# Linear attention fused with a capacity-routed mixture of experts: values loaded from ScalarE's queue, set-up work moved to VectorE's start, a new attention order, and digit counts folded by VectorE block transposes

## The chip, the cores and the metric

The kernel runs on one core of one Trainium2 chip. The metric is device time in microseconds (us) of one execution, given as the median of several runs; lower is better. The engines are PE (TensorE, matmuls; PEld is its weight load), DVE (VectorE), ACT (ScalarE), POOL (GpSimd) and SP (SyncE, which here only issues DMAs). A trailing q, as in SPq, marks DMA issues on that engine's queue. "Granted clock" is the share of TensorE's full clock that the profile records in a stretch; its two levels are 1.2 and 2.4 GHz, so 0.50 is the lower and 1.00 the upper one.

## The reference

Inputs: q, k, v of shape (8 batches, 8 heads, 576 positions, 64), a random-feature matrix w_phi (64 x 128), a gate (512 x 8) and the two weight matrices of 8 experts. What must be computed:

```python
def phi(x):
    proj = x @ w_phi
    proj = proj - max(abs(proj), axis=-1)
    return concat([exp(proj), exp(-proj)])
q_p, k_p = phi(q), phi(k)
kv  = einsum('bhsf,bhsd->bhfd', k_p, v);  z = k_p.sum(axis=2)
num = einsum('bhsf,bhfd->bhsd', q_p, kv); den = einsum('bhsf,bhf->bhs', q_p, z) + 1e-6
x = (num/den).transpose(0,2,1,3).reshape(4608, 512)
# routing: all 4608*8 logits in falling order; a token takes the expert of its highest
# logit whose expert is not yet full (576 tokens each)
logits = x @ w_gate
out[tokens of e] = maximum(x[tokens of e] @ w1[e], 0) @ w2[e]      # 512 -> 1024 -> 512
```

## The kernel before, in words

**Attention (0 to 296 us).** The 64 pairs of batch and head are worked in 16 units of four, u = 0 to 15 (two batches by two heads). Per unit SP issues 8 loads of k and 8 of q, 72 KB each (`raw` L115, its DMA line L122, called by `loadx`), two loads of v, 144 KB each (`loadv` L123, line L128), and one store of the finished block to `xs` in DRAM (L313). The loads write tiles with two buffers (`ki`, `qi`, `vi`). DVE turns k and q (`kT`, `qT`, L175); PE projects them (`g`, L186); DVE takes the row maximum (`kgm`, `qgm`, L190) and subtracts it (`kgt`, `qgt`, L193; two of the three k parts go by a copy on ACT L199 and a subtraction on POOL L202); ACT takes the exponentials (`kP`, L214). PE forms `kv` from `kP` and `vi` (L232), ACT copies it (`kvT` L236), PE spreads it by head (`bd` L248), and ACT copies it to `kz` (L251). POOL adds up the key features (`ks`, L222/L223), and PE and DVE place their sum in `kz` (L263, L265). PE transposes the query side (L276), ACT takes its exponentials (`qP`, L280), PE forms numerator and denominator ("num", L293), DVE divides (L297, L298, L308, tile `xp`), SP stores `xp`.

**What sets the order.** A planner written in Python, class `Plan` (L18), places every piece of a unit: each has an engine, a duration estimate, a due time, and buffer slots that it needs and frees. In the attention part each engine takes its pieces strictly by due time. The due times come from tables in the dictionary `ATT` (L913): `place` (L146) gives `u*16` plus the entry for the piece and engine from table '0' for the first unit, '1' for the second, '9' for the last and 's' for all between. The 19 pieces of set-up work for the routing (`init`, L336 to L342, which step through `moe_consts` L374: masks, iotas, selection matrices) have entries in table '0' that run from -103.6 to 91.2, so they lie scattered between the first units' work on DVE. The result of the planner is the program's order on each engine.

Each DMA goes on one of 8 completion lanes, given out in program order over all issuing engines; an issue first waits, on the engine that issues it, until the DMA before it on its lane has landed.

**Routing and experts (296 us to the end).** Routing finds, round by round, the expert that is filled next and the tokens that go to it. A round reads a 32-bit key in 6 digits (four of 5 bits, two of 6), from the top; for each digit it counts per expert how many tokens are at or above each of the K = 32 or 64 digit values, and finds the largest value at which the count still reaches the capacity. Round 0 is done in a wide form ahead of the experts. In rounds 1 to 6, which run beside the matmuls of experts 0 to 5, one digit is this chain: DVE compares (L586), PE counts with tokens packed n = 4 or 2 to a matmul (L602, 9 or 18 matmuls), DVE masks the packed result (`mm`, L604) and adds over n (`dd`, L606), PE adds over the n partition groups with a selection matrix (L609), DVE compares with the capacity (`fl`, L614), PE adds the flags over partitions (L616), DVE takes the digit (`ch`, L618) and moves to the next digit (`cc`, L622). The lines of one digit:

```python
mm=S([128,n,8],f'mm{n}'); V.tensor_mul(mm,p,msk[n])                     # L604
V.tensor_reduce(dd,mm.rearrange('p i e -> p e i'),axis=AX.X,op=OP.add)  # L606
p=rps([128,8]); PE.matmul(p,Q[n],dd[:,:,0],start=True,stop=True)        # L609
V.tensor_scalar(fl,p,float(cap),2.0**(-7*i),op0=OP.is_ge,op1=OP.mult)   # L614
p=rps([128,8]); PE.matmul(p,ones[0:KR],fl,start=True,stop=True)         # L616
```

An expert: weights arrive by DMA (`raww`, L736), ACT and DVE split them into a rounded part and a rest (`w1h` L804, `w1l` L807; `w2h`, `w2l` L808), POOL gathers the tokens (L819), PE transposes them (L824), then the two layers as three fp32r matmuls each (`h` L849, `y` L878 and L893) with ACT and DVE between (L860, L861, L864), and POOL scatters the result (L907). A second plan, with constants in `MOE` (L912), orders this part, the digits' steps with estimates from `steps` (L745).

Of the kernel before, what the change touches and what calls it, by code (L numbers as in the profile page):

```python
# [97 lines left out]
def attention(ctx, tc, nc, q, k, v, w_phi, w_gate, xs, L, C, xp, cfg={}, after=None, later=None, count=None, init=iter(())):  # L98
# [50 lines left out]
    def place(name,eng,u,due):  # L149
# [3 lines left out]
        return u*16.+t[{0:'0',1:'1',NU-1:'9'}.get(u,'s')][(name if isinstance(name,str) else ''.join(map(str,name)))+'.'+eng]  # L153
    def unit(u):
# [22 lines left out]
        def project(nm,g,s0,s1,due,src):  # L177
# [16 lines left out]
            add((nm,g),'PE',n*218.,due,pe,[(src[0]+'t',0),(src[0]+'t',1)],'Q',slots(('g',NG,nm,g)),((src,u),),ins=16*n+.5)  # L194
# [143 lines left out]
    for i in range(NI):  # L338
# [3 lines left out]
        P.add(('init',i),'DVE',330.,place(('init',i),'DVE',0,d['init']),some,[('init',i-1)] if i else [],lat=95.,after=3900.)  # L342
# [31 lines left out]
def moe_consts(rp, nc, C, L, MC, cfg={}):  # L374
# [599 lines left out]
```

## Time and profile before

| | |
|---|---|
| runs | 796.99, 798.92, 800.79 us; median 798.92 us |
| profiled execution | 796.87 us, span of its instructions 795.1 us, mean granted clock 0.978 |
| busy in the span | PE 750.4 us (94%), DVE 546.5 (69%), ACT 349.4 (44%), POOL 308.0 (39%) |
| attention, 0 to 296 us | 16 units |
| first routing round, 296 to 328 us | PE busy 20.1 of 32.4 us, granted clock 0.63 |
| experts 0 to 7, 328 us to the end | 62.6 us for expert 0; 57.6 to 58.8 for experts 1 to 5; 54.0 for expert 6 |

The span runs from the first to the last instruction; the execution's own time is 1.8 us longer. Busy shares are means over stages that have different limits, so each stage is to be read by itself.

### The profile page before, as it was taken

What the parts mean: (1) busy time and instruction counts of PE and PEld (TensorE: products, weight loads), DVE (VectorE), ACT (ScalarE), POOL (GpSimd) and SP (SyncE); (2) the same over time, 40 slices, a digit from 0 to 9 for tenths busy, and PEclk for the clock granted to TensorE, in tenths of its full rate; (3) what the DMA queues carried; (4) which work ended last, traced back from release to release, by engine and by line L of the source; (5) the groups of instructions that cost most, each with busy time, mean ns of one, the idle gap of its engine ahead of it and who ended that gap; (6) DMA issues with size and microseconds to landing.
All of it is one profiled execution on the core that took longest, in us unless ns stands there. A gap on an engine that the chain in (4) does not pass through costs nothing.

```text
span 795.1 us, 25101 instructions
## 1 busy us (share of the span) xinstructions
PE 750.4 (94%) x10718; PEld 651.2 (82%) x10718; DVE 546.5 (69%) x1343; ACT 349.4 (44%) x609; POOL 308.0 (39%) x327
## 2 busy tenths in 40 slices
PE   5999999899999986899999999999999999999995
PEld 3888888688888875598898898898898898897983
DVE  7998788598889857876686686685685685550400
ACT  2766667476766750343333333333333333441410
POOL 5887777688887850303203103104104104302011
PEclk9999999899999995899999999999999999999998
DMA  9767877867785311535505414423433334701200
GB/s 126 118 116 160 161 136 138 158 137 140 134 164 111 93 33 31 167 107 163 169 1 175 159 39 154 139 73 122 139 102 105 127 106 147 246 1 58 109 28 33
DMA packets 206655, 91.89 MB, mean 116 GB/s; under 512 B 154784, under 2 KB 189632, under 8 KB 206544
## 3 DMA queue, kind: packets, MB, share of 16 engines
q1 hardware_dynamic: 195712, 70.74, 37.5%
q0 software_dynamic: 6096, 18.97, 7.1%
q8 instruction: 84, 1.38, 0.7%
q10 hardware_dynamic: 4736, 0.59, 0.7%
q14 instruction: 27, 0.22, 0.1%
HBM read 71.39 MB, written 18.87 MB: 114 GB/s over the span
## 4 chain that ended last, share of the span: by engine, by line
PE 69%; issue 13%; DVE 5%; POOL 4%; SPq 3%; DMA 3%; ACT 1%; POOLq 0%; DVEq 0%; ACTq 0%
PE h L849 20%; PE y L878 17%; PE g L293 7%; PE g L232 7%; PE g L186 6%; SPq L122 3%; PE g L276 3%; PE y L893 2%; PE h L824 2%; POOL out_dram L907 1%; PE rps L602 1%; DMA qi<-in_q_dram 1%; POOL ks L223 1%; PE rps L598 1%; PE g L248 1%
## 5 line engine op out<-in xcount | busy, mean ns | idle before, releaser
L223 POOL TENSOR_TENSOR ks<-ks,kP 128x512 f32<-128x512 f32 x112 | 143.3, 1279 | 9.1 <-ACT kP L214 0.6
L849 PE MATMUL h<-xh,w1h 128*128 128x272 f32 (+3 forms) x512 | 144.5, 303 | 0.2 <-DVE xl L827 0.2
L849 PE MATMUL h<-xh,w1l 128*128 128x272 f32 (+3 forms) x512 | 142.9, 299 | 0.0
L907 POOL DMA_INDIRECT out_dram<-ysb,idx x40 | 40.4, 1010 | 206.2 <-ACT ysb L901 166.6
L860 ACT ACTIVATE fh<-h 128x272 fp32r<-128x272 f32 (+2 forms) x128 | 49.2, 384 | 134.7 <-PE h L849 123.6
L819 POOL DMA_INDIRECT xg<-xs,idx x40 | 39.5, 986 | 177.2 <-issue 141.3
L878 PE MATMUL y<-w2h,fl 128*128 128x512 f32 x256 | 102.1, 399 | 0.0
L878 PE MATMUL y<-w2l,fh 128*128 128x512 f32 x256 | 101.9, 398 | 0.0
L878 PE MATMUL y<-w2h,fh 128*128 128x512 f32 x256 | 101.3, 396 | 0.0
L849 PEld LDWEIGHTS h<-xh,w1h 128*128 128x128 f32 x512 | 96.4, 189 | 2.1 <-issue 1.2
L849 PEld LDWEIGHTS h<-xh,w1l 128*128 128x128 f32 x512 | 96.6, 189 | 0.0
L849 PE MATMUL h<-xl,w1h 128*128 128x272 f32 (+3 forms) x512 | 91.7, 298 | 0.0
L864 DVE SCALAR_TENSOR_TENSOR fl<-h,fh 128x272 fp32r<-128x272 f32 (+2 forms) x128 | 52.8, 420 | 55.8 <-ACT fh L860 42.4
L280 ACT ACTIVATE qP<-g 128x768 f32<-128x768 f32 x96 | 70.0, 828 | 41.9 <-PE g L276 41.9
L293 PE MATMUL g<-kz,qP 128*64 128x73 f32 x2304 | 78.5, 227 | 0.3 <-issue 0.3
L293 PEld LDWEIGHTS g<-kz,qP 128*64 128x64 f32 x2304 | 75.3, 136 | 3.7 <-issue 3.0
L214 ACT ACTIVATE kP<-kgt 128x768 f32<-128x768 f32 x96 | 72.7, 836 | 11.1 <-DVE kgt L193 10.5
L849 PEld LDWEIGHTS h<-xl,w1h 128*128 128x128 f32 x512 | 75.6, 188 | 0.0
L232 PE MATMUL g<-kP,vi 64*64 64x256 f32 x1152 | 73.2, 384 | 1.1 <-DVE xp L308 0.7
L901 ACT COPY ysb<-y 128x512 f32<-128x512 f32 (+1 forms) x40 | 21.8, 544 | 97.3 <-PE y L878 64.1
L232 PEld LDWEIGHTS g<-kP,vi 64*64 64x64 f32 x1152 | 44.1, 135 | 15.8 <-issue 3.9
L190 DVE TENSOR_REDUCE kgm<-g 128x6 f32<-128x768 f32 x48 | 44.5, 951 | 17.6 <-PE g L186 17.5
(195 smaller groups left out, 1340.1 us busy)
## 6 DMA issues: line engine op xcount, KB each, us to landing
raww<-in_moe_w_dram SPq DMA_DIRECT2D x64, 512.0 KB, 5.8
vi<-in_v_dram SPq DMA_DIRECT2D x32, 288.0 KB, 4.8
xs<-xp SPq DMA_DIRECT2D x16, 576.0 KB, 4.3
ki<-in_k_dram SPq DMA_DIRECT2D x124, 72.0 KB, 3.6
qi<-in_q_dram SPq DMA_DIRECT2D x124, 72.0 KB, 3.7
xg<-xs,idx POOLq DMA_INDIRECT x40, 3.5
out_dram<-ysb,idx POOLq DMA_INDIRECT x40, 2.9
ki<-in_k_dram ACTq DMA_DIRECT2D x4, 72.0 KB, 4.1
```

Of the source, the lines that this page charges most:

```text
L186: PE.matmul(p[64*bi:64*bi+64,a,128*(s-s0):128*(s-s0)+128],t[r,bi,s,:],C['w'][r,:],start=True,stop=True)
L190: V.tensor_reduce(m,vw(),axis=AX.X,op=OP.max,apply_absolute_value=True)
L214: for i in range(2): A.activation(o[:,:,:,128*i:128*i+128],t,AF.Exp,scale=1.0-2*i)
L223: else: G.tensor_add(ks,ks,kP[:,s])
L232: PE.matmul(p[64*a:64*a+64,i,0:256],v_[r,a,s,:],kP[r,s,a,:],start=s==0,stop=s==8,skip_group_check=True)
L280: for fh in range(2): A.activation(t[:,fh].rearrange('p a s t -> p a (s t)'),p,AF.Exp,scale=1.0-2*fh)
L293: PE.matmul(p[64*ab:64*ab+64,a,73*(j-j0):73*(j-j0)+73],T['qP',u,j//3][:,fh,a,j%3,64*ab:64*ab+64],T['kz',u][:,ab,fh,a,:],start=fh==0,stop=f ...
L849: PE.matmul(p,ws[:,k,o:o+128],xx[:,k,o1:o2],start=n==0,stop=n==11)
L860: A.activation(hh[:,f,o1:o1+m1],p[:,0:m1],AF.Relu)
L864: V.scalar_tensor_tensor(hl[:,f,o1:o1+m1],p[:,0:m1],0.0,hh[:,f,o1:o1+m1],op0=OP.max,op1=OP.subtract)
L878: PE.matmul(p,hx[:,f,o:o+128],ws[:,f%2,:],start=n==0,stop=n==23)
L907: st=G.indirect_dma_start(out=ov,out_offset=bass.IndirectOffsetOnAxis(ap=iv,axis=0),in_=yv,in_offset=None)
```

## The change

Four things are changed.

1. The two loads of v of every unit but the first are issued from ACT's queue, no longer from SP's; the planner's estimates for the loads' issue and landing rise a little.
2. `place` takes the due times of SP's pieces (loads and stores) from table 's' for every unit. All tables of `ATT` have new numbers, and so the pieces of a unit have a new order on every engine.
3. The 19 set-up pieces get due times of -100 to -82: they run first on DVE.
4. In the narrow rounds (1 to 6) the matmul with `Q[n]` is gone. DVE writes its sums over n into the first 8 of 32 columns of a tile `tin`, whose other columns are zero, transposes it in blocks of 32 x 32 (`tr`), adds over the n columns of a group (`cn8`), compares with the capacity (`f32`), adds the flags (`ds8`), and spreads that sum to one column per expert by a product with `eye8`, an 8-column diagonal made in the set-up. The matmul with ones follows as before. The estimates in `steps` and the constants in `MOE` change with it.

```diff
@@ loadv
-            nc.sync.dma_start(t[64*i:64*i+64].rearrange('p h s d -> p h (s d)'),o)
+            (nc.scalar if u else nc.sync).dma_start(t[64*i:64*i+64].rearrange('p h s d -> p h (s d)'),o)
@@ place
-        return u*16.+t[{0:'0',1:'1',NU-1:'9'}.get(u,'s')][(name if isinstance(name,str) else ''.join(map(str,name)))+'.'+eng]
+        return u*16.+t['s' if eng=='SP' else {0:'0',1:'1',NU-1:'9'}.get(u,'s')][(name if isinstance(name,str) else ''.join(map(str,name)))+'.'+eng]
@@ unit
-            add('ldk','SP',5200.,-d['ldk'],lambda x: loadx('k',k,u),slot=slots(('ki',2)),lat=4500.)
-            add('ldq','SP',5200.,-d['ldq'],lambda x: loadx('q',q,u),slot=slots(('qi',2)),lat=4500.)
-            add('ldv','SP',1300.,-d['ldv'],lambda x: loadv(u),slot=slots(('vi',2)),lat=4500.)
+            add('ldk','SP',6000.,-d['ldk'],lambda x: loadx('k',k,u),slot=slots(('ki',2)),lat=5000.)
+            add('ldq','SP',6000.,-d['ldq'],lambda x: loadx('q',q,u),slot=slots(('qi',2)),lat=5000.)
+            add('ldv','ACT',1300.,-d['ldv'],lambda x: loadv(u),slot=slots(('vi',2)),lat=5000.)
@@ set-up pieces
-        P.add(('init',i),'DVE',330.,place(('init',i),'DVE',0,d['init']),some,[('init',i-1)] if i else [],lat=95.,after=3900.)
+        P.add(('init',i),'DVE',270.,-100.+i,some,[('init',i-1)] if i else [],lat=95.,after=3900.)
@@ moe_consts
+    tin=rp.tile([128,32],F32,name='tin'); V.memset(tin,0.0)
+    eye8=rp.tile([128,8],F32,name='eye8')
+    V.tensor_reduce(eye8.rearrange('p (r o) -> p r o',o=1),ident.rearrange('p (q r) -> p r q',r=32)[:,0:8],axis=AX.X,op=OP.max)
@@ moe, one digit
                     mm=S([128,n,8],f'mm{n}'); V.tensor_mul(mm,p,msk[n])
-                    dd=S([128,8,1],'dd',F32R)
-                    with nc.allow_low_precision(reason='whole numbers under 2**13'): V.tensor_reduce(dd,mm.rearrange('p i e -> p e i'),axis=AX.X,op=OP.add)
+                    V.tensor_reduce(tin[:,0:8].rearrange('p (e o) -> p e o',o=1),mm.rearrange('p i e -> p e i'),axis=AX.X,op=OP.add)
+                    tr=S([128,32],'tr'); V.transpose(tr,tin)
                     yield
-
-                    p=rps([128,8]); PE.matmul(p,Q[n],dd[:,:,0],start=True,stop=True)
-                    yield
-                KR=K if wide else 128
-                fl=S([KR,8],f'fl{KR}',BF)
-                if part: V.scalar_tensor_tensor(fl,p,-float(cap),R['n0'],op0=OP.add,op1=OP.is_ge)
-                else: V.tensor_scalar(fl,p,float(cap),2.0**(-7*i),op0=OP.is_ge,op1=OP.mult)
+                    cn8=S([128,32//n,1],f'cn{n}'); V.tensor_reduce(cn8,tr.rearrange('p (k i) -> p k i',i=n),axis=AX.X,op=OP.add)
+                    f32=S([128,32//n],f'f{n}'); V.tensor_scalar(f32,cn8[:,:,0],float(cap),2.0**(-7*i),op0=OP.is_ge,op1=OP.mult)
+                    ds8=S([128,1],'ds'); V.tensor_reduce(ds8,f32,axis=AX.X,op=OP.add)
+                if wide:
+                    fl=S([K,8],f'fl{K}',BF)
...
+                else:
+                    fl=S([128,8],'fl128',BF); V.tensor_scalar(fl,eye8,ds8,None,op0=OP.mult)
                 yield
-                p=rps([128,8]); PE.matmul(p,ones[0:KR],fl,start=True,stop=True)
+                p=rps([128,8]); PE.matmul(p,ones[0:K] if wide else ones,fl,start=True,stop=True)
@@ tables
-MOE = {'TE': 57.0, 'stay': -0.21, ...
+MOE = {'TE': 50.56, 'stay': 1.77, ...
```

How the order of instructions moves at the places that matter. First DVE at the start of the program, from the constants to the first unit's `kgt`; the rows name the line, the operation, output and input. Before, from the transposes of k:

```order
L175 STREAM_TRANSPOSE kT<-ki 128x2x288 x2
L424 TENSOR_REDUCE ms_190<-ident 128x2
L425 COPY msk_188<-ms_190 128x16
L427 TENSOR_REDUCE Q_189<-ident 128x64
L428 TENSOR_SCALAR Q_189<-jp 128x64
L190 TENSOR_REDUCE kgm<-g_193 128x6
L190 TENSOR_REDUCE kgm<-g_208 128x6
L193 TENSOR_TENSOR kgt<-g_193,kgm 128x768
```

and in the change, from the second half of k:

```order
L175 STREAM_TRANSPOSE kT<-ki 128x2x288
L433 CAST dup<-Q_177 128x64 x2
L437 TENSOR_SCALAR dup_218<-dup,msk_176 128x128 x2
L442 TENSOR_SCALAR idp<-idi 128x36
L443 TENSOR_SCALAR idp<-idi 128x36
L444 CAST ids<-idp 128x72
L447 TENSOR_REDUCE half<-ident 128x1
L452 TENSOR_REDUCE eye_236<-ident 128x8
L175 STREAM_TRANSPOSE qT<-qi 128x2x288
L190 TENSOR_REDUCE kgm<-g_205 128x6
L175 STREAM_TRANSPOSE qT<-qi 128x2x288
L193 TENSOR_TENSOR kgt<-g_205,kgm 128x768
```

All set-up work now stands ahead of the first `kgm`; before, most of it came later, between the work of units 0 to 3.

Next the ACT queue where unit 1's values are loaded, with what each instruction waits for in brackets (DMAHW0 to DMAHW7 are the lanes). Before, the exponentials of unit 1:

```order
L199 COPY kgt<-g_427 128x768 [waits DVE_49,Activation_49]
L199 COPY kgt<-g_444 128x768 [waits DVE_49,Activation_49]
L214 ACTIVATE kP<-kgt 128x2x3x128 [waits Pool_49]
L214 ACTIVATE kP<-kgt 128x2x3x128
L214 ACTIVATE kP<-kgt 128x2x3x128 [waits DVE_49]
```

and in the change:

```order
L214 ACTIVATE kP<-kgt 128x2x3x128 [waits Pool_49]
L214 ACTIVATE kP<-kgt 128x2x3x128
L128 DMA vi<-in_v_dram 64x2x576 [waits DMAHW0_49]
L128 DMA vi<-in_v_dram 64x2x576 [waits DMAHW2_49]
L199 COPY kgt<-g_499 128x768 [waits DVE_49,PE_49]
L214 ACTIVATE kP<-kgt 128x2x3x128 x2
```

and SP's queue in the change at the end of unit 3's k and through unit 3's q:

```order
L122 DMA ki<-in_k_dram 32x18x32 [waits DMAHW0_49]
L122 DMA ki<-in_k_dram 32x18x32 [waits DMAHW1_49]
L122 DMA qi<-in_q_dram 32x18x32 [waits DMAHW2_49,DVE_49]
L122 DMA qi<-in_q_dram 32x18x32 [waits DMAHW3_49]
L122 DMA qi<-in_q_dram 32x18x32 [waits DMAHW4_49]
L122 DMA qi<-in_q_dram 32x18x32 [waits DMAHW5_49]
L122 DMA qi<-in_q_dram 32x18x32 [waits DMAHW6_49]
L122 DMA qi<-in_q_dram 32x18x32 [waits DMAHW7_49]
L122 DMA qi<-in_q_dram 32x18x32 [waits DMAHW1_49]
L122 DMA qi<-in_q_dram 32x18x32 [waits DMAHW3_49]
L122 DMA ki<-in_k_dram 32x18x32 [waits DMAHW4_49,DVE_49]
```

The two loads of v now stand in ACT's queue between exponentials of unit 1. In SP's round of lanes, 0 and 2 are passed over behind unit 3's sixth q load: those two turns are the v loads'. So the first v load follows the seventh k load of unit 3 on lane 0, and the second follows the first q load of unit 3 on lane 2.

Last, one digit on DVE in the expert part, before:

```order
L604 TENSOR_TENSOR mm_7930<-rps,msk_422 128x32
L606 TENSOR_REDUCE dd<-mm_7930 128x8
L808 TENSOR_TENSOR w2l_7924<-raww_7828,w2h_7923 128x512
L614 TENSOR_SCALAR fl_7946<-rps 128x8
L808 TENSOR_TENSOR w2l_7924<-raww_7828,w2h_7923 128x512
L618 TENSOR_REDUCE ch<-rps 128x1
L622 SCALAR_TENSOR_TENSOR cc<-cc,ch,dg 128x36
```

and in the change:

```order
L607 TENSOR_TENSOR mm_8033<-rps,msk_183 128x32
L608 TENSOR_REDUCE tin<-mm_8033 128x8
L609 STREAM_TRANSPOSE tr<-tin 128x32
L813 TENSOR_TENSOR w2l_7980<-raww_7883,w2h_7979 128x512
L611 TENSOR_REDUCE cn_8051<-tr 128x8
L612 TENSOR_SCALAR f_8053<-cn_8051 128x8
L613 TENSOR_REDUCE ds<-f_8053 128x1
L619 TENSOR_SCALAR fl_8057<-eye_236,ds 128x8
L869 SCALAR_TENSOR_TENSOR fl<-h_7996,fh 128x272
L813 TENSOR_TENSOR w2l_8008<-raww_7908,w2h_8007 128x512
L623 TENSOR_REDUCE ch<-rps 128x1
```

Four DVE instructions are added to each digit (the block transpose, `cn`, `f` and `ds`), and `fl` reads them, not a PE result; PE's matmul between `dd` and `fl` is gone, on 36 digits in all.

## Rows read from the trace of the kernel before

**Rows 1.** The page's busy times, and its chain of work that ended last.

```profile
PE 750.4 (94%) x10718; PEld 651.2 (82%) x10718; DVE 546.5 (69%) x1343; ACT 349.4 (44%) x609; POOL 308.0 (39%) x327
...
PE 69%; issue 13%; DVE 5%; POOL 4%; SPq 3%; DMA 3%; ACT 1%; POOLq 0%; DVEq 0%; ACTq 0%
```

**Rows 2.** Busy times from one unit's num start to a later one's; last columns: clock, DMA share, GB/s.

```profile
core 0: us, PE busy (x) PEld busy (x) DVE busy (x) ACT busy (x) POOL busy (x), PEclk, DMA share, GB/s
50.42:68.30 17.88, 16.16 (x446) 14.40 (x442) 16.07 (x28) 11.97 (x18) 13.70 (x12) 1.00 0.67 118
...
136.50:159.85 23.35, 19.34 (x448) 16.85 (x446) 14.26 (x22) 11.74 (x17) 14.29 (x14) 0.85 0.80 155
...
175.97:192.09 16.12, 16.01 (x444) 14.22 (x446) 14.20 (x22) 11.55 (x17) 13.46 (x11) 1.00 0.77 147
...
243.00:261.05 18.05, 16.91 (x430) 14.62 (x426) 16.51 (x36) 11.60 (x17) 13.60 (x12) 1.00 0.56 124
...
275.97:291.35 15.38, 15.38 (x375) 13.44 (x377) 9.00 (x15) 9.84 (x14) 12.66 (x13) 1.00 0.14 42
```

**Rows 3.** Timeline of SP, then of DVE, ahead of 147 us: start, duration, instruction, [idle before].

```profile
128.21 13.68 SPq L122 DMA_DIRECT2D qi<-in_q_dram  x16
...
145.88 0.91 DVE L308 TENSOR_TENSOR xp<-g,rd 128x720 f32<-128x720 f32 x1 [5.36 <-DMA xs<-xp]
```

**Rows 4.** Timeline of DVE (two set-up pieces), then of ACT (units 0 and 1).

```profile
47.40 2.07 DVE L437 TENSOR_SCALAR dup<-dup,msk 128x128 bf16<-128x128 bf16 x2
...
64.18 1.44 DVE L442 TENSOR_SCALAR idp<-idi 128x36 int32<-128x36 int32 x1 [0.86 <-POOL idi L441]
...
16.05 1.58 ACT L214 ACTIVATE kP<-kgt 128x768 f32<-128x768 f32 x2 [5.17 <-DVE kgt L193]
...
31.19 1.58 ACT L214 ACTIVATE kP<-kgt 128x768 f32<-128x768 f32 x2
```

**Rows 5.** Timeline of SP: loads of units 1 and 3; the page's DMA issues (us to landing last).

```profile
23.65 1.74 SPq L128 DMA_DIRECT2D vi<-in_v_dram  x2
...
38.53 6.01 SPq L122 DMA_DIRECT2D ki<-in_k_dram  x8
...
vi<-in_v_dram SPq DMA_DIRECT2D x32, 288.0 KB, 4.8
...
ki<-in_k_dram SPq DMA_DIRECT2D x124, 72.0 KB, 3.6
```

**Rows 6.** Timeline of ACT's queue at the start: four loads of the first unit's q.

```profile
3.97 5.60 ACTq L122 DMA_DIRECT2D qi<-in_q_dram  x4
```

**Rows 7.** Timeline of PE: unit 1's first kv matmuls, and its num.

```profile
39.05 2.82 PE L232 MATMUL g<-kP,vi 64*64 64x256 f32 x48 [0.33 <-DVE xp L308]
...
50.42 0.79 PE L293 MATMUL g<-kz,qP 128*64 128x73 f32 x18
```

**Rows 8.** Busy times of experts 0, 4 and 6; columns as in rows 2.

```profile
328.40:391.00 62.60, 61.05 (x472) 52.87 (x473) 47.34 (x148) 23.37 (x47) 9.69 (x15) 1.00 0.42 134
...
566.30:624.40 58.10, 58.10 (x447) 50.49 (x447) 40.02 (x124) 19.92 (x42) 10.28 (x16) 1.00 0.34 114
...
682.00:736.00 54.00, 54.00 (x347) 47.92 (x347) 19.29 (x37) 19.80 (x42) 8.58 (x14) 1.00 0.27 96
```

**Rows 9.** Timeline of PE around one matmul with Q (L609) in expert 5.

```profile
627.86 0.17 PE L609 MATMUL rps<-dd,Q 128*128 128x8 f32 x1
627.89 0.37 PE L849 MATMUL h<-xh,w1h 128*128 128x272 f32 x1
628.10 0.29 PE L849 MATMUL h<-xh,w1l 128*128 128x272 f32 x1
628.23 0.29 PE L849 MATMUL h<-xl,w1h 128*128 128x272 f32 x1
```

**Rows 10.** DVE groups by line and form (busy, mean ns), then a wait of DVE.

```profile
L175 DVE STREAM_TRANSPOSE kT<-ki 128x576 f32<-128x576 f32 x32 | 23.2, 761 | 0.0
...
L606 DVE TENSOR_REDUCE dd<-mm 128x8 fp32r<-128x32 f32 x24 | 5.1, 211 | 0.8
...
DVE fl L614 <- PE rps L609: 10.5, 13, 3.1
```

More of the change, by code (lines that the diff above doesn't have):

```diff
@@ L193, in sub @@
                 V.tensor_sub(t,vw(),T[nm+'m',u,g].to_broadcast([128,2,n,128]))
-            add((nm,g),'PE',n*218.,due,pe,[(src[0]+'t',0),(src[0]+'t',1)],'Q',slots(('g',NG,nm,g)),((src,u),),ins=16*n+.5)
+            add((nm,g),'PE',n*(218. if not first else 480. if nm=='kg' else 340.),due,pe,[(src[0]+'t',0),(src[0]+'t',1)],'Q',slots(('g',NG,nm,g)),((src,u),),ins=16*n+.5)
             add((nm+'m',g),'DVE',dv(256*n),due+.8,mx,[(nm,g)])
@@ L541, in state @@
         return dict(m=S([128,NT,1],'m'),dg=S([128,ND,NT],'dg',BF),sm=S([128,NT,1],'sm',BF),OH=S([128,NT,8],'OH',BF))
-    MC.extend((state,prep,(cmp0,cnt0,put0,prep0),DIG,KW,kt,kl,scl,k0,e8,ones,tri,dif,onef,msk,Q,dup,dup2,ids,half,un,opn,spacer))
+    MC.extend((state,prep,(cmp0,cnt0,put0,prep0),DIG,KW,kt,kl,scl,k0,e8,ones,tri,dif,onef,msk,Q,dup,dup2,ids,half,un,opn,spacer,tin,eye8))
 def moe(ctx, tc, nc, L, xs, w1, w2, out, C, MC, R0, cfg={}):
@@ L555, in mid @@
     def mid(x,t): return x[:,None,:].to_broadcast([x.shape[0],t,x.shape[1]])
-    state,prep,(cmp0,cnt0,put0,prep0),DIG,KW,kt,kl,scl,k0,e8,ones,tri,dif,onef,msk,Q,dup,dup2,ids,half,un,opn,spacer=MC
+    state,prep,(cmp0,cnt0,put0,prep0),DIG,KW,kt,kl,scl,k0,e8,ones,tri,dif,onef,msk,Q,dup,dup2,ids,half,un,opn,spacer,tin,eye8=MC
     ND=len(DIG)
@@ L604, in routing @@
                     mm=S([128,n,8],f'mm{n}'); V.tensor_mul(mm,p,msk[n])
-                    dd=S([128,8,1],'dd',F32R)
-                    with nc.allow_low_precision(reason='whole numbers under 2**13'): V.tensor_reduce(dd,mm.rearrange('p i e -> p e i'),axis=AX.X,op=OP.add)
+                    V.tensor_reduce(tin[:,0:8].rearrange('p (e o) -> p e o',o=1),mm.rearrange('p i e -> p e i'),axis=AX.X,op=OP.add)
+                    tr=S([128,32],'tr'); V.transpose(tr,tin)
                     yield
-                    p=rps([128,8]); PE.matmul(p,Q[n],dd[:,:,0],start=True,stop=True)
-                    yield
-                KR=K if wide else 128
-                fl=S([KR,8],f'fl{KR}',BF)
-                if part: V.scalar_tensor_tensor(fl,p,-float(cap),R['n0'],op0=OP.add,op1=OP.is_ge)
-                else: V.tensor_scalar(fl,p,float(cap),2.0**(-7*i),op0=OP.is_ge,op1=OP.mult)
+                    cn8=S([128,32//n,1],f'cn{n}'); V.tensor_reduce(cn8,tr.rearrange('p (k i) -> p k i',i=n),axis=AX.X,op=OP.add)
[3 more added lines that the diff above has]
+                    fl=S([K,8],f'fl{K}',BF)
+                    if part: V.scalar_tensor_tensor(fl,p,-float(cap),R['n0'],op0=OP.add,op1=OP.is_ge)
+                    else: V.tensor_scalar(fl,p,float(cap),2.0**(-7*i),op0=OP.is_ge,op1=OP.mult)
+                else:
+                    fl=S([128,8],'fl128',BF); V.tensor_scalar(fl,eye8,ds8,None,op0=OP.mult)
                 yield
-                p=rps([128,8]); PE.matmul(p,ones[0:KR],fl,start=True,stop=True)
+                p=rps([128,8]); PE.matmul(p,ones[0:K] if wide else ones,fl,start=True,stop=True)
                 if r: yield
@@ L754, in steps @@
                 if i: z+=[('DVE',820*(2 if two else 1))]
-                z+=[('PE',(450 if two else 230)+130,'A'),('DVE',400),('PE',110,'A'),('DVE',160),('PE',110,'A')]
+                z+=[('PE',(450 if two else 230)+130,'A'),('DVE',600),('DVE',650),('PE',110,'A')]
                 if i<ND-1: z+=[('DVE',450)]
```

4 lines of the change are left out of this document (2 added, 2 removed).

## The prediction

> **What bounds the kernel now.** I read the page's busy times and chain first, then busy times by stage, then timelines where a stage is slower than its neighbours. PE is busy for 94% of the span and makes up 69% of the chain [rows 1], so a change pays only where PE stands still or loses a matmul. Read by unit, from one unit's numerator matmuls (num) to the next unit's, an undisturbed unit takes 16.12 us with PE busy for 16.01 of them [rows 2]: nothing but PE sets it. Two kinds of unit are longer. The early one at 50 us takes 17.88 us, with DVE busy for 16.07 of it and PE for only 16.16: part of DVE's load there is set-up work, for instance the 1.44 us piece at 64.18 that also waited 0.86 us for POOL [rows 4]. The stretch of 23.35 us at 136.50 holds a stall [rows 2]: SP issued 16 loads of q in one row, 13.68 us, and the store of a finished block had to stand behind them, so that DVE waited 5.36 us for that store to free a buffer [rows 3]; PE's mean clock over the stretch fell to 0.85. That stretch alone is 7.2 us over the undisturbed unit. In the expert part PE is full: 58.10 of 58.10 us in expert 4; only expert 0 has 1.55 us of idle PE [rows 8].
>
> **Start.** All set-up work is moved ahead of the first row maximum. It is the 2.07 us pair of masks, the 1.44 us id piece [rows 4], about a dozen small pieces at the 0.21 us of a small reduction (2.5 us), and half a transposed q at 0.76 us [rows 10]: 6.8 us. Some of it fits into the time in which DVE waits for PE's first projection, so I take 5.5 us for what reaches the path, with 4 to 7 as ends. The first exponentials go from 16.05 to 21.5 us, and unit 1's from 31.19 to 36.7 [rows 4].
>
> **Values on ACT's queue, unit 1.** Behind unit 1's first exponentials (two of 0.8 us, done at 38.3) ACT now issues the two v loads. The order says on which lanes they go: the first behind the seventh k load of unit 3, the second behind the first q load of unit 3, both on SP's queue. When do those land? Before, k of unit 3 went out from 38.53 for 6.01 us, behind a pair of v loads of 1.74 us [rows 5] that is now gone, so it starts at about 36.7. Its seventh load is issued at 41.2 and, at the 3.6 us that a k load takes to land [rows 5], is there at 44.8; the first load of q goes out at 42.8 and lands at 46.4. So ACT stands from 38.3 to 46.4, 8 us, with four more k exponentials and two copies of unit 1 behind the load; POOL waits for those with its sums, and PE for the values. The values land 4.8 us after issue [rows 5], at about 51.5. From unit 1's first kv matmul to its num PE needs 50.42 - 39.05 = 11.4 us [rows 7], which gives 63; by ACT's remaining exponentials (at 47 now, before about 33, which was 17.5 us ahead of num) it gives 64.8. I take num of unit 1 at 64, against 50.42 before. That ACT's queue can be held by landings is seen at the start: four q loads took 5.60 us to issue there [rows 6], where SP issues eight in 6.01 [rows 5].
>
> **From unit 2 on.** By then SP has run ahead by its v loads and the loads come well before their use, so lanes should be free when ACT reaches its v loads. SP loses 1.74 us per unit [rows 5], which ACT gains; ACT is busy for 11.55 of 16.12 us [rows 2], so it fits. SP's pieces now have the same place in every unit, so no 16 loads in a row come before a store, and that stall goes; late next is PE itself. The set-up work is gone from the units around 50 us. Routing's preparation stays (the 18.05 us unit at 243.00, DVE 16.51 busy [rows 2]). For the twelve periods from unit 1's num to unit 13's I take 16.35 us each: ten near the undisturbed 16.12 and two a little over 17. Before, they took 261.05 - 50.42 = 210.6 us; now 196.2. So unit 13's num comes at 64 + 196.2 = 260.2, before at 261.05 [rows 2]; the last units (15.38 for the last period [rows 2]) stay as they are. **Attention: -1 us**, ends -5 (periods of 16.1, num at 62) and +6 (16.75, num at 65).
>
> The Trainium skill ("DMA: Bandwidth & Descriptors", section Issuing engines are not separate DMA queues) says that loads started from several engines still share the same DMA engines, and that only the sequencer's issue time is saved. By that rule alone the move of v would be worth at most the 1.74 us per unit on SP, which is not on PE's path in an undisturbed unit, so nothing; the sum by it would be the same but for the hold-up. The same page (section Anatomy of one DMA) says that a wait for a semaphore is spent on the issuing sequencer before dispatch, which agrees with the 5.60 us on ACT's queue [rows 6].
>
> **Digits.** Thirty-six matmuls with Q leave PE. One starts at 627.86; the second matmul behind it starts at 628.10, 0.24 us later, where the next step is 0.13 [rows 9]: it cost 0.11 us, or 4.0 us for 36. The low end: experts 4 and 6 differ by 100 matmuls and 4.1 us [rows 8], 0.041 each, 1.5 us for 36. The high end: its own 0.17 us [rows 9], 6.1 us. I take 4.0 since it is read at the matmul itself. DVE gets four small instructions per digit, about 0.21 us each by the small reduction, at most 0.76 for the transpose by the large one [rows 10]: 0.84 us per digit, 5 us per expert. In expert 4 DVE goes from 40 to 45 of 58 us: hidden beside PE. If that cover were gone, all 30 us could show. The round does not get longer by it: the hop to PE that goes cost `fl` 10.5 us in 13 waits, 0.8 each [rows 10]. Only in expert 0, where DVE is busy for 47.34 us and the splits of weights that PE needs stand between the digits, do I charge 1.5 us, with 0 and 4 as ends. **Experts: -2.5 us.**
>
> **Sum.** -1 - 2.5 = -3.5 on the profiled execution's 796.87 us gives 793.4. That execution lies 2.05 us under the median of 798.92, so on the scale of the median I forecast 795.4 us. What a measurement can tell from no change is about 0.5%, 4 us.
>
> **Rivals.** *ACT is not held.* If the lanes are free when ACT comes to unit 1's v loads, num of unit 1 is only as late as the start, 55.9, and 8 us come back: 787.4. For it: SP issues k and q without visible waits [rows 5]. Against it: the lane order given above, and the 5.60 us at the start [rows 6].
>
> *ACT's queue becomes a link of each unit's chain, and the kernel is slower.* The v loads stand between exponentials and the copy of kv, which PE's next matmuls wait for. PE idles for only 0.11 us of an undisturbed unit [rows 2], so what is late on ACT shows in full once its lead there is used up. If half the pair's issue time of 1.74 us [rows 5] reaches PE in each of twelve periods, 10.4 us are added: 805.8. It decides from about 0.3 us per unit on (12 x 0.3 eats the gain). For it: ACT's issues wait for landings [rows 6]. Against it: ACT's 4.6 idle us per unit.
>
> *The fold takes back what the matmuls give.* PE loses a matmul but DVE becomes late with weight splits and digits. Then the experts give 0 and the sum is -1: 797.9. For it: expert 0's DVE load [rows 8]. Against it: 18 idle us of DVE in expert 4. The Trainium skill ("VectorE: DVE Perf Modes", section Rules for kernel authors) speaks for this one: it asks for few DVE instructions and calls the reduction the slowest, and the fold adds four, two of them reductions. The trace bears it out only as far as 0.21 us for a small reduction [rows 10] against 18 us of room.
>
> **Chances.** My own chain .50: 795.4, itself between 791 and 800, which is about as often past the 0.5% as not. ACT not held .22, ACT in each unit's chain .20, fold takes it back .08. Faster by over 0.5%: .22 + .23 = .45; slower: .20; within 0.5%: .35. The range leaves out the far half of the slower case and the best of the unheld one: 785 to 804.5.
>
> **What would show it.** Right: first exponentials of k at 21 to 22 us; an idle stretch of 7 us or more on ACT before it goes on with unit 1, and PE waiting for `vi` near 45 to 51; num of unit 1 at 62 to 65; no stall near 140 us; units of 16.1 to 16.5; expert 4 at 57.3 to 57.6 us; DVE about 5 us busier per expert. Wrong: num of unit 1 before 58; units of 16.8 or more with PE waiting for `kvT`, `kz` or `vi`; a new wait of the store; expert 0 above 64 us, or experts 1 to 5 no shorter than before.

## The result, and the profile after

The changed kernel takes 791.47 us (median of 20 runs, 788.80 to 795.78), the kernel before 798.50 us beside it (20 runs, 793.48 to 803.55). The ratio is 0.9916, with a 95% interval from 0.9898 to 0.9934: 6.7 us faster, 5.3 to 8.1. The forecast was 795.4 us, 3.5 us faster, with a range from 785 to 804.5.

The profiled execution took 791.46 us, span 789.7 us. Its busy times and its chain, from the page, beside [rows 1]:

```profile
PE 743.3 (94%) x10682; PEld 645.6 (82%) x10682; DVE 567.5 (72%) x1489; ACT 352.4 (45%) x609; POOL 305.7 (39%) x327
...
PE 72%; issue 12%; DVE 7%; DMA 2%; SPq 2%; POOL 2%; ACT 1%; POOLq 0%; ACTq 0%; DVEq 0%
```

PE has 36 matmuls fewer and is busy for 7.1 us less; DVE has 146 instructions more and is busy for 21 us more. The chain is still PE's.

**The start.** Busy times of the change by stretch, columns as in [rows 2]: the stop of PE and what follows it, then two later units, and the last period.

```profile
core 0: us, PE busy (x) PEld busy (x) DVE busy (x) ACT busy (x) POOL busy (x), PEclk, DMA share, GB/s
36.00:44.60 8.60, 0.30 (x11) 0.15 (x7) 4.35 (x8) 0.85 (x2) 0.00 (x0) 0.66 0.62 107
44.60:50.50 5.90, 5.90 (x80) 5.59 (x84) 1.63 (x4) 3.74 (x6) 5.64 (x5) 0.62 1.00 176
62.28:78.43 16.15, 16.10 (x443) 14.30 (x442) 14.70 (x23) 11.97 (x17) 14.78 (x12) 1.00 0.75 146
176.61:193.69 17.08, 16.59 (x443) 14.61 (x442) 14.53 (x23) 12.34 (x18) 13.65 (x13) 1.00 0.76 144
275.20:289.83 14.63, 14.63 (x368) 12.80 (x367) 8.62 (x17) 8.11 (x12) 10.92 (x11) 1.00 0.15 43
```

The timeline of ACT (its first exponentials, then at that stop) and its queue, then of PE (start, duration, instruction, idle time before):

```profile
17.30 1.58 ACT L214 ACTIVATE kP<-kgt 128x768 f32<-128x768 f32 x2 [7.04 <-DVE kgt L193]
...
31.19 1.58 ACT L214 ACTIVATE kP<-kgt 128x768 f32<-128x768 f32 x2 [0.52 <-POOL kgt L202]
41.47 2.17 ACTq L128 DMA_DIRECT2D vi<-in_v_dram  x2
43.74 0.80 ACT L199 COPY kgt<-g 128x768 f32<-128x768 f32 x1 [10.98 <-DMA qi<-in_q_dram]
...
33.54 2.76 PE L293 MATMUL g<-kz,qP 128*64 128x73 f32 x80
44.60 4.16 PE L293 MATMUL g<-kz,qP 128*64 128x73 f32 x64 [8.30 <-ACT kgt L199]
...
62.28 1.93 PE L293 MATMUL g<-kz,qP 128*64 128x73 f32 x54
```

ACT finishes unit 1's first exponentials at 32.8 us and then does nothing for 10.98 us: its next two instructions are the v loads, and by the order of lanes they can't be issued until two loads on SP's queue have landed. PE stops in the middle of unit 0's num, because the copy of `kgt` that stands behind the v loads on ACT is what frees its next result buffer. The mean granted clock is 0.62 in the 5.9 us behind the stop. This is the hold-up that was forecast; only PE meets it earlier, through a copy and not through the values. Num of unit 1 comes at 62.28 us, 11.9 us later than before [rows 7].

From there the twelve periods to unit 13 take 197.3 us (62.28 to 259.62), against 210.6 before, with eight of them at 16.15 to 16.18 us. The stall at 146 us [rows 2, 3] is gone. The last num starts at 289.83 us, before at 291.27 (PE's own row; [rows 2] cut the stretch at 291.35).

**The experts.** Busy times from one expert's last matmul of `y` to the next one's; expert 0 from its first `h`. First the change (experts 0, 1, 4, 6), then the kernel before with the same ends (experts 0, 1, 4, 6):

```profile
327.69:389.45 61.76, 60.69 (x462) 51.88 (x462) 49.89 (x171) 23.19 (x46) 9.16 (x14) 1.00 0.38 123
389.45:446.72 57.27, 57.27 (x442) 49.84 (x441) 43.90 (x149) 20.18 (x42) 10.83 (x15) 1.00 0.36 121
...
561.24:618.49 57.25, 57.25 (x441) 49.84 (x441) 43.76 (x149) 20.08 (x42) 10.29 (x15) 1.00 0.35 114
...
676.09:729.50 53.41, 53.41 (x342) 47.32 (x343) 23.40 (x47) 19.52 (x42) 10.31 (x15) 1.00 0.28 100
```

```profile
328.37:390.32 61.95, 60.40 (x467) 52.28 (x467) 46.69 (x146) 23.00 (x46) 9.72 (x15) 1.00 0.42 130
390.32:448.53 58.21, 58.21 (x448) 50.89 (x448) 42.24 (x131) 20.14 (x42) 11.00 (x15) 1.00 0.34 109
...
565.23:623.34 58.11, 58.11 (x447) 50.50 (x446) 40.02 (x124) 19.92 (x42) 10.29 (x15) 1.00 0.34 114
...
681.50:734.84 53.34, 53.34 (x342) 47.26 (x341) 19.29 (x37) 19.80 (x42) 8.16 (x13) 1.00 0.26 91
```

Experts 1 to 5 get shorter by 0.9 us on average (0.6 to 1.3; expert 4 goes from 58.11 to 57.25), in PE time, while DVE is 3.7 us busier in expert 4; expert 6, which has no digits, is unchanged. From the first `h` (328.37 before, 327.69 now) to the end of the span the experts take 466.7 us before and 462.0 now.

So the span's 5.4 us come out as 1.4 in attention, 4.7 in the experts, and 0.8 lost between them, where PE waited 1.4 us for gathered tokens and before 0.8. How far this split holds in other executions is read below, with the parts side by side: the experts' share holds, the attention's does not stand out. The medians differ by 1.6 us more than these two executions: the profiled execution of before is that much under the median of its 20 runs.

### The profile page after: what moved, and what is told of

Its sections match the earlier page's. It is cut to its first block, busy times and chain, and to the rows that moved or that the text cites. A ratio compares the mean times of both kernels' runs of the same rounds, so it can differ in the third digit from the quotient of the medians.

```text
span 789.7 us, 25148 instructions
## 1 busy us (share of the span) xinstructions
PE 743.3 (94%) x10682; PEld 645.6 (82%) x10682; DVE 567.5 (72%) x1489; ACT 352.4 (45%) x609; POOL 305.7 (39%) x327
## 4 chain that ended last, share of the span: by engine, by line
PE 72%; issue 12%; DVE 7%; DMA 2%; SPq 2%; POOL 2%; ACT 1%; POOLq 0%; ACTq 0%; DVEq 0%
PE h L854 19%; PE y L883 16%; PE g L293 9%; PE g L232 7%; PE g L186 6%; PE g L276 4%; PE y L898 3%; SPq L122 2%; PE h L829 2%; PE rps L605 1%; PE g L248 1%; PE rps L601 1%; POOL out_dram L912 1%; DMA qi<-in_q_dram 1%; PE g L263 1%
## 5 line engine op out<-in xcount | busy, mean ns | idle before, releaser
L854 PE MATMUL h<-xh,w1h 128*128 128x272 f32 (+3 forms) x512 | 142.4, 300 | 0.3 <-DVE xl L832 0.3
L214 ACT ACTIVATE kP<-kgt 128x768 f32<-128x768 f32 x96 | 75.5, 840 | 20.1 <-DVE kgt L193 11.0
L280 ACT ACTIVATE qP<-g 128x768 f32<-128x768 f32 x96 | 72.4, 809 | 20.9 <-PE g L276 11.3
L232 PE MATMUL g<-kP,vi 64*64 64x256 f32 x1152 | 70.3, 377 | 0.5 <-DVE kgt L193 0.5
L883 PEld LDWEIGHTS y<-w2h,fh 128*128 128x128 f32 x256 | 48.2, 188 | 9.2
L883 PEld LDWEIGHTS y<-w2l,fh 128*128 128x128 f32 x256 | 48.2, 188 | 9.0
```

The costliest lines, as they stand in the source:

```text
L214: for i in range(2): A.activation(o[:,:,:,128*i:128*i+128],t,AF.Exp,scale=1.0-2*i)
L232: PE.matmul(p[64*a:64*a+64,i,0:256],v_[r,a,s,:],kP[r,s,a,:],start=s==0,stop=s==8,skip_group_check=True)
L280: for fh in range(2): A.activation(t[:,fh].rearrange('p a s t -> p a (s t)'),p,AF.Exp,scale=1.0-2*fh)
L854: PE.matmul(p,ws[:,k,o:o+128],xx[:,k,o1:o2],start=n==0,stop=n==11)
L883: PE.matmul(p,hx[:,f,o:o+128],ws[:,f%2,:],start=n==0,stop=n==23)
```

## The experiments

Ratios are to runs of the kernel before on the same chip, with the 95% interval. The change had 0.9916 in the comparison above and 0.9906 (0.9873 to 0.9939) in a second one, g2 below.

**Is it ACT's queue?** The change, with the v loads of unit 1 issued at the start, where ACT is idle:

```diff
     loadv(0)
+    loadv(1)
-            add('ldv','ACT',1300.,-d['ldv'],lambda x: loadv(u),slot=slots(('vi',2)),lat=5000.)
+            if u==1: P.add(('ldv',1),'X',0.,-90.,lambda x: None,slot=slots(('vi',2)))
+            else: add('ldv','ACT',1300.,-d['ldv'],lambda x: loadv(u),slot=slots(('vi',2)),lat=5000.)
```

> The changed kernel with one difference: ACT issues the two v loads of unit 1 at the very start, behind its loads of q, and not between unit 1's exponentials; all other orders are the same. Theory A (ACT's queue was held from 32.8 to 43.7 us by these two issues, which waited for SP's loads on their lanes, and PE's 8.3 us stop at 36.3 us followed from it): no stop of PE inside unit 0's num matmuls, unit 1's num starts at 51 to 54 us, not 62.3, later periods unchanged at 16.15, and the time is 8 to 11 us under the changed kernel's, 781 to 784 us. Rival B (the stop has another cause, such as the k loads of unit 3 themselves, or PE waits elsewhere for the 8 us): num of unit 1 stays at 60 us or later and the time within 3 us of the changed kernel's.

Measured: 0.9916 (0.9889 to 0.9943), 793.32 us, no faster than the change. Timeline of ACT's queue and ACT, then of PE:

```profile
55.34 1.70 ACTq L128 DMA_DIRECT2D vi<-in_v_dram  x2
57.08 0.59 ACT L238 COPY kvT<-g 128x512 f32<-128x512 f32 x1 [11.28 <-DMA ki<-in_k_dram]
...
33.52 4.79 PE L295 MATMUL g<-kz,qP 128*64 128x73 f32 x144
...
57.72 1.24 PE L250 MATMUL g<-bd,kvT 64*64 64x72 f32 x32 [9.26 <-ACT kvT L238]
...
64.12 2.07 PE L295 MATMUL g<-kz,qP 128*64 128x73 f32 x42
```

Theory A holds for the first stop, unit 0's num runs through, and fails on the time, 781 to 784 us. ACT comes to the v loads of unit 2 so much earlier, and stands there for 11.28 us, now behind k loads of SP's. Num of unit 1 is at 64.12. The hold-up isn't a property of one load: ACT's v loads can't run ahead of the loads on SP's queue with which they share the lanes, and SP's queue is behind.

**Does SP have room?** The change with all v loads back on SP:

```diff
-            (nc.scalar if u else nc.sync).dma_start(...)
+            nc.sync.dma_start(...)
-            add('ldv','ACT',1300.,...
+            add('ldv','SP',1300.,...
-'ldv.ACT': 23.676,
+'ldv.ACT': 23.676, 'ldv.SP': 50.0,
```

> The changed kernel with all v loads back on SP's queue, behind the k loads of the next unit; PE's, DVE's and POOL's orders are as in the changed kernel. Theory A (what the change gains in attention comes from the regular places and the new order, and ACT's queue only costs its 11 us hold-up): PE's stop at 36 us is gone, unit 1's num starts at 51 to 55 us, the periods stay at 16.15 to 16.8 because SP's issues fit into a unit (16 loads at about 0.7 us, a store 0.6, two v loads 1.7: about 14 of 16.15 us), time 781 to 785 us. Rival B (SP has no room for v, which is why v was moved): the store of a block is late again, DVE waits for it for some us per unit, periods of 16.8 or more, time 790 us or more.

Measured: 0.9974 (0.9951 to 0.9997), 797.97 us, 4.6 us slower than the run of e1 beside it. Both theories hold, each for a while. Num of unit 1 starts at 52.12 us and the units follow at 16.15 to 16.55 us up to 198 us. Then SP is late. PE's row of that num, SP's queue later on, and DVE's longest wait from 190 to 300 us:

```profile
52.12 4.79 PE L293 MATMUL g<-kz,qP 128*64 128x73 f32 x144
```

```profile
195.11 8.57 SPq L122 DMA_DIRECT2D qi<-in_q_dram  x8
203.78 5.86 SPq L122 DMA_DIRECT2D ki<-in_k_dram  x8
209.74 2.62 SPq L128 DMA_DIRECT2D vi<-in_v_dram  x2
212.46 0.55 SPq L313 DMA_DIRECT2D xs<-xp  x1
213.11 6.94 SPq L122 DMA_DIRECT2D qi<-in_q_dram  x8
...
228.73 8.74 SPq L122 DMA_DIRECT2D qi<-in_q_dram  x8
```

```profile
DVE qT L175 <- DMA qi<-in_q_dram: 15.0, 4, 6.3
```

Each of the first five rows starts 0.1 us behind the end of the one before, and so do those left out. A row of several loads can hide waits inside it, as the one on ACT's queue at the start does [rows 6], where four issues of 0.57 us fill 5.60; taken one by one, these 38 issues take 0.55 to 1.94 us each, 31.5 us in all, and no gap between two of them is over 0.1 us: the queue is not idle. Why some issues take twice as long or more as the usual 0.63 us is not shown. Two units take it from 195.11 to 228.73, 16.8 us each, where PE asks for one every 16.15. It starts with a lead and uses it up over some ten units. So SP's queue is a second bound of the attention part, close under PE, and moving v away is what keeps the loads on time in the change.

**The stall at 146 us.** The kernel before, with the last unit's q loads in the place that the other units have:

```diff
-'9': {'ldk.SP': -10.469, 'ldq.SP': -106.932, ...
+'9': {'ldk.SP': -10.469, 'ldq.SP': 1.917, ...
```

> The kernel before with one number changed: the q loads of the last unit take the place that the other units' q loads have, so that SP no longer issues 16 q loads in one row at 128 us. Theory A (the 13.7 us row kept the store behind it, and that made the 23.35 us stretch): the wait of DVE for the store at 146 us is gone, the stretch comes to about 16.5 us, the kernel is 6 to 7.5 us faster than before, 791 to 792.5 us on the scale of 798.5. Rival B (the lost time was owed elsewhere too, such as loads that then come late): under 3 us.

Measured: 1.0142 (1.0109 to 1.0175), 810.43 us, 10 us over the median of before beside it: neither. DVE's first wait from 190 to 300 us:

```profile
DVE qT L175 <- DMA qi<-in_q_dram: 17.3, 1, 17.3
```

The wait for the store is gone, but the last q is now issued at the end of a full queue, and DVE waits 17.3 us for it. Loading it early was a reserve against just that. The lost time was owed elsewhere, and more of it than rival B thought.

**Set-up first.** The kernel before with set-up due at -150 and up:

```diff
-        P.add(('init',i),'DVE',330.,place(('init',i),'DVE',0,d['init']),some,...
+        P.add(('init',i),'DVE',270.,-150.+i,some,...
```

> The kernel before with the 19 set-up pieces moved ahead of everything else on DVE, as in the change, and nothing else. Theory A (packed at the start, while POOL is idle, the same pieces cost about 3 us of DVE against some 8 us scattered between work of POOL): first num 2 to 3 us later than the 31.2 us before, the mask pair takes 0.4 to 0.5 us in place of 2.07, units 1 to 3 take 1 to 2 us less each than their 19.2, 17.9 and 17.9 us, so the kernel is 0 to 3 us faster than before. Rival B (the early units are long for another reason): num of unit 3 is 2 us or more later than before's 86.2 and the kernel 2 to 3 us slower.

Measured: 1.0002 (0.9979 to 1.0024), 799.57 us: nothing. The pieces do become short (the mask pair 251 ns each in place of 1,074, the id piece 175 ns in place of 1,444), and num of unit 0 comes 4.2 us later, at 35.41, more than theory A allowed. By unit 3 (86.57, before 86.13) the loss is nearly made up, and nothing is left over. That fits a queue of loads that sets the pace and is no faster than it was; it was not tried apart.

**Which part of the expert change?** The kernel before with the fold alone (the diff's lines of `moe_consts`, `moe` and `steps`), and with the fold and the new `MOE` constants:

> The kernel before with the fold of the digit counts alone (its lines, its two constants, its duration estimates), with the old attention and the old constants of the expert plan. Theory A (the 36 matmuls with Q cost PE 0.11 to 0.15 us each and the four extra DVE instructions per digit are hidden): experts 1 to 5 at 57.2 to 57.6 us each in place of 58.1 to 58.6, kernel 3.5 to 5 us faster than before. Rival B (the new constants of the plan made the gain): within 1.5 us of before. Rival C (DVE becomes late): expert 0 over 63 us and no gain.

> The kernel before with the fold and the new constants of the expert plan, old attention. Theory A: as the fold alone, within 1 us of it. Rival B (the plan's constants carry the gain): 3 us or more faster than the fold alone.

Measured: the fold alone 1.0044 (1.0026 to 1.0062), 804.29 us, 3.4 us slower than before; with the new constants 0.9868 (0.9841 to 0.9896), 789.91 us, and in a second run (g3) 0.9900 (0.9871 to 0.9928), 792.54 us. Expert 1 of the fold alone, and PE's longest waits in it, then expert 1 of the fold with the constants:

```profile
390.37:455.21 64.84, 59.72 (x445) 51.97 (x447) 47.37 (x158) 21.10 (x44) 10.72 (x15) 0.95 0.29 96
```

```profile
PE rps L621 <- DVE fl L619: 2.3, 1, 2.3
PE rps L605 <- DVE cmp L589: 2.1, 1, 2.1
```

```profile
388.39:445.65 57.26, 57.26 (x442) 49.83 (x441) 43.89 (x149) 20.07 (x42) 10.83 (x15) 1.00 0.38 119
```

With the old constants PE comes to the matmul with ones 2.3 us before DVE has `fl` ready, and in the same expert to a count (L605) 2.1 us before DVE has its compare ready, and stands each time. Expert 1 takes 64.84 us and not 57.26; 5.1 of the 7.6 us are idle PE, the rest is PE work at a mean granted clock of 0.95. So theory A is right on the size of the saving and wrong that the fold alone brings it; rival B is right that the constants decide. Whether they bring a gain of their own was not run: the new constants without the fold are in no experiment, and f3 below only shows that, with the fold in, one matmul per digit put back leaves the expert part 0.2 to 2.1 us under the old one.

**What does a matmul with Q cost?** The change with one put back per digit, its result unused:

```diff
-                    p=rps([128,n,8])
+                    pq=rps([128,n+1,8]); p=pq[:,0:n,:]
...
                     tr=S([128,32],'tr'); V.transpose(tr,tin)
                     yield
+                    PE.matmul(pq[:,n,:],Q[n],Q[n][:,0:8],start=True,stop=True,skip_group_check=True)
```

> The changed kernel with one matmul with Q per digit added back on PE at the place in which the old one stood (between the digit's sums and its flags), its result unused, all other orders the same. Theory A: 36 times 0.11 to 0.15 us, so 4 to 5.4 us slower than the changed kernel. Rival B (the gain was in the shorter chain of hops, not in PE's time): within 1.5 us of the changed kernel.

Measured: 0.9925 (0.9897 to 0.9954), 795.06 us; the interval, 2.3 us either way, takes in the change's own ratio, so the time alone doesn't tell; its middle lies 0.7 to 1.5 us behind the change's two, nearer to rival B. The profile tells. Expert 3:

```profile
506.91:564.91 58.00, 58.00 (x446) 50.56 (x446) 44.04 (x149) 20.05 (x42) 10.32 (x15) 1.00 0.34 116
```

58.00 against 57.25 us: 0.75 us for 6 digits, 0.125 us each, 4.5 us for 36. The whole stretch says the same: from the first `h` to the end 466.5 us, in the change 462.0. Theory A on PE's time; the median didn't show all of it.

**Is DVE's added work hidden?** The change with the fold's four instructions done twice:

```diff
-                    tr=S([128,32],'tr'); V.transpose(tr,tin)
+                    tr=S([128,32],'tr'); V.transpose(tr,tin); V.transpose(tr,tin)
...
+                    for _ in range(2):
                         cn8=...; f32=...; ds8=...
```

> The changed kernel with the four instructions of the fold done twice in each digit, 4 x 36 more DVE instructions of some 0.16 to 0.21 us, about 27 us of DVE. Theory A (hidden beside PE): experts 1 to 5 unchanged within 0.1 us, expert 0 up to 1.5 us longer, kernel at most 2 us slower than the changed one. Rival C (DVE is at its limit): 4 us per expert, 20 us or more slower.

Measured: 1.0142 (1.0114 to 1.0170), 811.92 us, about 18 us slower than the change. Expert 2, and PE's longest wait in the expert part up to 640 us:

```profile
451.33:511.90 60.57, 58.03 (x439) 50.31 (x440) 47.25 (x174) 20.15 (x42) 10.41 (x15) 1.00 0.32 109
```

```profile
PE rps L622 <- DVE fl L620: 10.0, 21, 0.8
```

An expert takes 3.3 us more, 0.55 us per digit, of the some 0.73 us that the four instructions take (212, 182, 172 and 161 ns in the change). DVE is busy for 47 of 60.6 us and not at its limit, so rival C's reason is wrong, but its size is near. Of the 3.3 us PE is idle for 2.5: what the added time meets is PE's matmul with ones, which stands where the plan expects the fold to be over. In the change the cover is there, and it is thin: about 0.2 us per digit, what is left of 0.73 when 0.55 reach PE.

**The parts side by side.** The attention part alone, the change, the fold with the plan, and this last one with the last unit's q loads one place later, behind the store:

```diff
-'9': {'ldk.SP': -10.469, 'ldq.SP': -106.932, ...
+'9': {'ldk.SP': -10.469, 'ldq.SP': -106.0, ...
```

> The kernel before with the attention part of the change alone (v on ACT's queue, set-up first, new places and order); digits and expert plan as before. Theory A (the two profiles: last num 1.4 us earlier, the 8.3 us stop at 36 us in place of the stall at 146 us): 0 to 3 us faster than before. Rival B (the digits and the expert plan carry all of the gain, and the attention part gives back some of it, as the fold with the plan measured 0.9868 alone and the whole change 0.9916): 2 to 5 us slower than before.

> The changed kernel itself, beside the others on one chip: 0.990 to 0.994 of before, as measured. If the attention part costs (rival B of the run before), it is 2 us or more slower than the fold with the plan; if it gives (theory A), it is as fast or faster.

> The fold with the new constants of the expert plan, old attention, again, beside the change: 0.985 to 0.992 of before; under the changed kernel by 2 us or more if the attention part costs time.

> The fold with the new plan, old attention, and one number changed so that SP issues the last unit's q loads just behind the store and no longer ahead of it; all other orders are the same. Theory A (the store behind 16 loads made the stall at 146 us, and the last unit's q must still come early since SP's queue is full): DVE's wait for the store there goes from 5 us to under 1, the stretch comes to 17 us or less, no late q at the end, kernel 2 to 6 us faster than the fold with the plan, 783 to 788 us if that is at 790. Rival B (SP's queue is full in any order, and the lost time comes back in the following units): within 1.5 us of it.

Measured: attention alone 0.9978 (0.9954 to 1.0003), 797.56 us; the change 0.9906, 791.86 us; fold and plan 0.9900, 792.54 us; with the q loads behind the store 0.9846 (0.9814 to 0.9879), 789.13 us. Attention alone is 1.8 us faster with an interval that just takes in no change at all, in line with theory A. The expert part alone gives 8 us here and 10.6 us in f2, more than the profiles' 4.7; whether the whole change is faster or slower than it is not settled by these intervals.

The profiled executions tell the two parts apart. From the first `h` to the end of the span, the seven with the change's experts (the change, e1, e2, f2, g2, g3, g4) take 462.0 us within 0.1, the four with the old ones (before, e3, e4, g1) 466.7 to 468.6: the expert part is worth 4.7 to 6.6 us, clear of the scatter. Attention is not clear of it. The last num starts at 287.8 to 291.0 us in the five with the change's attention part (the change, f3, f4, g1, g2) and at 288.2 to 291.3 in the four with the old one (before, f1, f2, g3). So the 1.4 us of one pair are no proof of a gain there: the hold-up of ACT and the stall that went come out about even as far as these executions show, and the gain that these runs show is the experts'. What f2 and g3 gain beyond that is not explained.

The run with the q loads behind the store beats the kernel before, and in its median the change too; its interval overlaps with the change's, and with that of f2, the same kernel without the moved loads. SP's timeline, then PE's busy times in that stretch and the next:

```profile
124.56 8.74 SPq L122 DMA_DIRECT2D qi<-in_q_dram  x8
133.40 0.58 SPq L313 DMA_DIRECT2D xs<-xp  x1
134.08 6.98 SPq L122 DMA_DIRECT2D qi<-in_q_dram  x8
```

```profile
137.20:155.45 18.25, 16.36 (x446) 14.42 (x443) 13.99 (x22) 13.08 (x19) 15.23 (x15) 1.00 0.68 118
155.45:171.57 16.12, 16.01 (x444) 14.22 (x443) 14.43 (x22) 10.04 (x15) 12.91 (x12) 1.00 0.74 150
```

No wait for the store is left in it (3.0 us in f2, 5.4 in g3), the early q is kept, and the stretch is 18.25 us (18.80 and 21.96). That is theory A's mechanism, though the stretch didn't come to 17; its size, 4.3 us against g3 and 1.8 against f2 by the ratios, is not settled.

## Why the prediction was right, and where it was off

The direction and most of the mechanism were right; the measured gain is nearly twice the forecast 3.5 us. In the two profiled executions 2.2 us of the difference are the experts'; attention with the routing behind it gave 0.7 where 1 was forecast, and 1.6 us are the scale. That attention came out so near is in part luck: num of unit 1 was 1.7 us earlier than forecast and the twelve periods 1.1 us longer.

- **ACT held in unit 1: right.** Forecast: from 38.3 to 46.4, 8 us, num of unit 1 at 64. Measured: 10.98 us up to 43.74, num at 62.28. That PE would wait for the values themselves was wrong; it waited for a copy behind them. Both ends of the wait lie earlier than forecast: ACT was free at 32.8 us, since unit 1's first exponentials were not late at all (31.19 in both kernels), and its two issues were through 2.7 us sooner.
- **Start: mis-sized.** The 5.5 us for the set-up work were 1.25 us at the first exponentials (16.05 to 17.30) and 2.4 at num of unit 0 (31.18 to 33.54). I had priced the mask pair and the id piece at their scattered durations [rows 4], 3.5 of the 6.8 us; packed at the start they take 0.42 and 0.18 us. The first units do get shorter without the set-up work (by 1.5, 1.5 and 0.8 us in e4), and the later start takes that back.
- **From unit 2 on: right in size, incomplete in cause.** Twelve periods were forecast at 196.2 us and took 197.3; the last num is 1.4 us earlier in this pair, where 1 was forecast, and the other executions scatter by more than that. But "late next is PE itself" is only half of it: SP's queue lies right behind PE (e2, e3), which the prediction read as a queue without visible waits.
- **The rival "ACT is not held", 787.4 us:** it would not have given its 8 us by freeing one load. e1 did that, and the hold-up moved to the next.
- **Digits: right in size, wrong in cover.** 0.11 us per matmul forecast, 0.125 measured (f3). "Hidden beside PE" by 18 idle us of DVE was the wrong measure: f4 shows that 0.55 of a further 0.73 us per digit reaches PE. (DVE got 3.7 us busier in each of experts 2 to 5, where 5 was forecast.) The third rival had the right wait at the wrong place; the plan's new constants, which I costed at nothing, are what keeps it out.
- **Experts: the term that was off.** Forecast -2.5 us, measured -4.7, and up to -6.6 by the other executions. Of the 1.5 us charged to expert 0 about 0.5 came (it is 0.2 us shorter, where its six matmuls would give 0.7), and experts 1 to 5 gain 0.9 us each on average where 6 x 0.11 = 0.66 was taken. Of that 0.9 the matmuls are 0.75 (f3); the rest is open.
- **The scale.** I added the 2.05 us by which the profiled execution lay under the median to the forecast of the change as well. Of before it was 1.6 us against 20 runs, of the change nothing. The wait for the store at 146 us, which the change doesn't have, was 3.0 us in f2's execution and 5.4 in those of before and g3, so some of that scatter may be the stall's; that was not tried. Some of it lies in the experts: of the four executions with the old experts, that of before has the shortest expert part (466.7 of 466.7 to 468.6 us).
- **Two sums** are off without moving the forecast: 47 + 17.5 is 64.5 and not 64.8, and the ends of attention come to -5.9 and +5.0 by the values in the brackets, not to -5 and +6.

## What to carry to other kernels

A queue that issues loads is an engine with a busy share of its own: add up the durations of its issues over a unit before calling another engine the bound, and look whether gaps are left between them, also inside a row that stands for several. Moving a load to a second engine's queue doesn't make it independent where, as here, the two share completion lanes; the issue waits on the engine that holds it, with all that stands behind it. And where an in-order engine waits for a chain on another, what hides longer work in the chain is the place of the waiting instruction, not the idle share of the engine that does the work: a cheaper chain and the plan that places it are one change.

## What the runs showed of the hardware that was not expected

**The same DVE instruction took four to eight times as long beside POOL.** Timelines of before (DVE, then POOL) and, in the second fence, of the change (DVE):

```profile
64.18 1.44 DVE L442 TENSOR_SCALAR idp<-idi 128x36 int32<-128x36 int32 x1 [0.86 <-POOL idi L441]
...
46.52 2.90 POOL L202 TENSOR_TENSOR kgt<-kgt,kgm 128x768 f32<-128x768 f32 x2 [2.05 <-PE g L276]
...
64.12 1.46 POOL L202 TENSOR_TENSOR kgt<-kgt,kgm 128x768 f32<-128x768 f32 x1
```

```profile
13.07 0.42 DVE L437 TENSOR_SCALAR dup<-dup,msk 128x128 bf16<-128x128 bf16 x2
13.40 0.18 DVE L442 TENSOR_SCALAR idp<-idi 128x36 int32<-128x36 int32 x1
```

The id piece lasts 1.44 us while POOL's subtraction runs from 64.12 for 1.46 us, and 0.18 us when POOL is idle; the mask pair is 2.07 us, from 47.40 [rows 4], beside POOL's two subtractions up to 49.42, and 0.42 without. The Trainium skill ("SBUF — State Buffer", section SBUF: two separate sides) says that VectorE and GpSimd share one pair of ports as an exclusive lock, for some VectorE instructions, and that the loser waits for the whole instruction. The ends of these rows agree with that; in which mode the instruction runs no row here shows.

**The clock at the start, by execution.** In the change PE stands for 7.46 us ahead of its first projections, where it stood for 6.17 before. In the profiled execution of the change the granted clock then goes to its lower level; in that of e1, with the same idle time of PE, it does not (busy times by stretch, of the change and of e1):

```profile
10.00:12.00 2.00, 0.01 (x1) 0.05 (x1) 1.93 (x9) 0.26 (x1) 0.00 (x0) 0.50 1.03 202
```

```profile
10.00:12.00 2.00, 0.01 (x1) 0.04 (x1) 1.93 (x9) 1.28 (x1) 0.00 (x0) 1.00 0.99 182
```

The clock was low there in g2's execution too, and at its upper level in those of e2, f3, f4 and g1. It made no difference to the time: num of unit 0 starts between 33.51 and 33.56 us in all seven, and PE waits for DVE ahead of it in all of them.
